# A weight conversion in two VectorE operations and a sloped ScalarE function, for three and an absolute value, in an attention and two-layer MLP kernel

## The chip, the cores and the metric

One core of a Trainium2 chip runs the whole program. The metric is the device time of one execution in microseconds (us); the median over the runs of a kernel is compared. The kernel before takes 915.51 us (three runs, 914.54 to 918.71).

## What is computed

Four batches of eight heads attend over 576 positions of width 64: the first four heads see the last 32 positions, the other four see positions that are a multiple of 32 back. The output, 2304 tokens by 512, goes through two blocks of two matrix products each (512 to 2048 to 512).

```python
attn_out = _attn_ref(q, k, v)                 # softmax over masked scores
x = attn_out as (2304, 512)
h = x @ moe_w_in
g = where(h >= 1, h, where(h <= -1, 0, (h + 1)**2 / 4))
x = g @ moe_w_out
h = x @ moe2_w_in
g = s * relu(h)**2 + b
return g @ moe2_w_out
```

The four weight matrices arrive as 64-bit floats. The core has no such type, so each weight is read as two 32-bit words and its 32-bit float is put together on chip: the high word, read as a float and multiplied by 2 to the power -112, has the right exponent bits three places too low, so that it has to be shifted left by three, and the top three bits of the low word come in below.

## The kernel before, in words

A product runs as three passes over TensorE, since each operand is a high part and a remainder (hi times hi, hi times lo, lo times hi). So each weight tile of 128 by 512 is converted to a 32-bit float (tile `wc`), then split: ScalarE copies it to the rounded type (`w_parts`, line 700, or `w_combine`, line 707, for the last matrix), and GpSimd subtracts the copy from it. There are 64 such tiles: 32 of the first block, loaded while the attention still runs, and 32 of the second, loaded late in the first block.

The conversion stands in `w_abs` (line 677) and `w_bits` (line 682). `w_abs` takes a PSUM bank `c` and lets ScalarE write |high word| times 2^-112 there. `w_bits` takes one of three buffers `wc` and issues three VectorE operations: `c` shifted left by three with the sign bit masked off, in place in PSUM; the low word shifted right by 29 and or-ed in, again in place; and the sign of the high word or-ed in, the result to `wc`. The words lie 8 bytes apart in the loaded tile `wr`.

Nothing is issued in the order of the program text. The class `Order` records every operation with a time (`nc.now`, in slots of one layer-1 or layer-2 step), and `issue` (line 267) then lays them out when the program is built: it keeps a modelled clock for each engine, and whenever an engine comes free it takes, of the operations whose inputs the model says are ready, the one with the lowest recorded time. `price` (line 228) gives the modelled duration: a VectorE operation is charged half as much per column if `fast` (line 249) holds, a scalar operation with all operands in SBUF, and `port` (line 252) says which VectorE operations the model lets wait for GpSimd's and the other way round: those that are `fast` and those with two full inputs (`whole`) in SBUF. The resulting order in each engine's queue is fixed in the program. The SyncE queue (SP), which issues nearly all DMAs, is laid out in the same way; the model lets it run at most 12 us ahead of the modelled transfers (line 354). Idle time of TensorE up to the first layer-1 step is filled, at build time, with matmuls on zeros (`idle`).

```python
        return op in ("tensor_scalar", "tensor_scalar_add", "tensor_copy") and not any(self.in_psum(x) for x in aps)
...
        return self.fast(op, aps) or len(whole) > 1
...
                free[e] = max(free[e], dma - DMA_AHEAD)
```

Around the conversions run, on VectorE, ScalarE and GpSimd: the softmax of the attention units (`s`, `mx`, `sm`, `pt`), the split of the tokens (`x_split`, line 788: `xh` by ScalarE, `xl` by VectorE or GpSimd), the activation between the layers (`activate`, line 846: `u` and `g` from the PSUM bank `h`), and the copies of a finished block of tokens (`finish`, line 957): `o` is copied from the PSUM bank `y` into one of three buffers that `u` uses as well, and SP writes it out (`x<-o`). In the second block `combine` (line 871) and `finish_fast` (line 908) do this with sums and differences of quarter blocks.

Of the kernel before, what the change touches and what calls it, by code (L numbers as in the profile page):

```python
# [12 lines left out]
F32 = mybir.dt.float32  # L13
F32R = mybir.dt.float32r
BF16 = mybir.dt.bfloat16
I32 = mybir.dt.int32
AF = mybir.ActivationFunctionType
ALU = mybir.AluOpType
# [15 lines left out]

DROP = -1.0e30

REBIAS = 2.0 ** -112

# [344 lines left out]
def attention_moe_moe(ctx, tc, q, k, v, w1_in, w1_out, w2_in, w2_out, s_in, b_in, consts, out):  # L385
    nc = Order(tc.nc)
# [268 lines left out]
    wt, wraw, wtags, reserved, used = {}, {}, {}, {}, {}  # L655

    def w_load(ph, f, x):
        w = ((w1_in, w1_out), (w2_in, w2_out))[ph][x]
        if ph == 0:
            tag = f"w{f}_{x}"  # L660
        else:
            tag = reserved[f // 2].pop(0) if x else rooms.pop(0)
        wtags[ph, f, x] = tag

        r = wraw[ph, f, x] = nc.tile(sb, [P, DM, 2], I32, tag=tag, name=f"wr{ph}_{f}_{x}")
        if x == 0:
            nc.sync.dma_start(
                out=r.rearrange("p (c m) w -> p c (m w)", m=P),
                in_=w[:, 2 * f * P:2 * (f + 1) * P].rearrange("(c p) m -> p c m", p=P),
            )  # L670
        else:
            nc.sync.dma_start(out=r.rearrange("p m w -> p (m w)"), in_=w[f * P:(f + 1) * P, :])


    wc = {}

    def w_abs(ph, f, x):
        c = nc.bank(ps, W_BANKS if now[0] < 2 * NP * NBLK - 4 else W_BANKS_FAST, f"c{ph}_{f}_{x}", "c")
        nc.scalar.activation(out=c, in_=wraw[ph, f, x][:, :, 1].bitcast(F32), func=AF.Abs, scale=REBIAS)
        wc[ph, f, x] = c  # L680

    def w_bits(ph, f, x):
        c, r = wc[ph, f, x].bitcast(I32), wraw[ph, f, x]
        o = wc[ph, f, x] = nc.tile(sb, [P, DM], I32, tag="wc", bufs=WC_BUFS, name=f"wc{ph}_{f}_{x}")
        nc.vector.tensor_scalar(
            out=c, in0=c, scalar1=3, scalar2=0x7FFFFFFF, op0=ALU.logical_shift_left, op1=ALU.bitwise_and
        )
        nc.vector.scalar_tensor_tensor(
            out=c, in0=r[:, :, 0], scalar=29, in1=c, op0=ALU.logical_shift_right, op1=ALU.bitwise_or
        )  # L690
        nc.vector.scalar_tensor_tensor(
            out=o, in0=r[:, :, 1], scalar=-0x80000000, in1=c, op0=ALU.bitwise_and, op1=ALU.bitwise_or
        )

    def w_room(tag, name, width=DM):
# [36 lines left out]
    def plan_w(f):  # L732
        for x in range(2):
            first, step, apart = W_TIMES[f // (NF // 2)]
            t = first + step * (f % (NF // 2)) + apart * x
            at(t - W_AHEAD, w_load, 0, f, x)
            at(t, w_abs, 0, f, x)
            at(t, w_bits, 0, f, x)
            at(t + 0.3, w_parts, 0, f, x)

# [6 lines left out]
    def half_split(tag):  # L747
        t = nc.tile(sb, [P, 2, 2, HM], F32R, tag=tag, name=f"halves_{tag}")
        for i in range(2):
            halves[tag, i] = t[:, i]  # L750
            half_rooms.append((tag, i))

    def pump():
        while todo and todo[0][0] <= nc.now and nc.now >= loaded[0] + W_GAP:
            ph, f, x = tile = todo[0][1]
            p = f // 2
            if x and f % 2 == 0:
                if not half_rooms and len(rooms) > 4 and p >= HP:
                    half_split(rooms.pop(0))
                if len(rooms) < 4 or not half_rooms:  # L760
                    break
                reserved[p] = [rooms.pop(0) for _ in range(4)] + [half_rooms.pop(0)]
            elif not x and not rooms:
                break
            todo.pop(0)
            loaded[0] = nc.now
            w_load(*tile)
            t = nc.now + W_AHEAD
            at(t, w_abs, *tile)
            at(t, w_bits, *tile)  # L770
            if not x:
                at(t + 0.3, w_parts, *tile)
            elif f % 2:
                at(t + 0.3, w_combine, p)
        if todo:
            at(max(nc.now + W_RETRY, todo[0][0]), pump)
# [219 lines left out]
    def at(time, fn, *args):  # L996
        heapq.heappush(events, (time, next(planned), fn, args))
# [41 lines left out]
    with tc.manual_schedule():  # L1039
# [17 lines left out]
        for f in range(NF):  # L1057
            plan_w(f)
        at(todo[0][0], pump)

        run(-1)
# [57 lines left out]
```

## Time and profile before

| | us |
|---|---|
| median of three runs (lowest, highest) | 915.51 (914.54, 918.71) |
| the profiled execution's own time | 914.73 |
| its span, first to last instruction | 913.0 |
| TensorE busy | 886.8 (97%) |
| VectorE busy | 523.3 (57%) |
| ScalarE busy | 495.9 (54%) |
| GpSimd busy | 414.1 (45%) |
| mean granted TensorE clock | 0.987 of full speed |

The busy times are sums over the span; they don't add up, since the engines run side by side. What lies outside the span (1.7 us) is start and end of the execution.

### The profile page before, as it was taken

To read this page: it belongs to the slowest core of one execution; us is meant where nothing else is said; L and a number is where in the kernel's file an instruction comes from. 1 tells how busy PE (TensorE), PEld (TensorE's weight loads), DVE (VectorE), ACT (ScalarE), POOL (GpSimd) and SP (SyncE) were. 2 spreads that over 40 slices of the span, in tenths; PEclk is the share of its full clock that TensorE was granted. 3 is DMA by queue.
4 is the path that set the end of the run, shared out by engine and by line. 5 is a ranking of instruction groups with operands and counts; after the bars stand their busy time and mean duration, and the time that the engine had idled before them with its cause. 6 is when DMAs were issued, how large, how long until landed. Compare 5 with 4: busy or idle time off the path is not lost.

```text
span 913.0 us, 22147 instructions
## 1 busy us (share of the span) xinstructions
PE 886.8 (97%) x8922; PEld 872.8 (96%) x8922; DVE 523.3 (57%) x1057; ACT 495.9 (54%) x1097; POOL 414.1 (45%) x350
## 2 busy tenths in 40 slices
PE   8987999999999999999999999999999999999996
PEld 7987999999999999999999999999999899999996
DVE  2787686443443342333696888744457965455455
ACT  2676677545444443233554687665666655555553
POOL 4174454122222112222354577987645665545544
PEclk9999799999999999999999999999999999999999
DMA  9899322422222211002635743445134332222211
GB/s 161 258 300 309 89 75 71 103 52 52 64 52 63 53 61 70 1 24 70 209 127 172 232 140 116 145 136 183 70 115 164 98 129 99 94 93 93 94 47 47
DMA packets 122966, 103.37 MB, mean 113 GB/s; under 512 B 84272, under 2 KB 100976, under 8 KB 122864
## 3 DMA queue, kind: packets, MB, share of 16 engines
q1 hardware_dynamic: 122352, 100.85, 36.7%
q0 software_dynamic: 512, 1.11, 0.6%
q8 instruction: 70, 1.15, 0.5%
q14 instruction: 32, 0.26, 0.1%
HBM read 73.63 MB, written 28.31 MB: 112 GB/s over the span
## 4 chain that ended last, share of the span: by engine, by line
PE 87%; DMA 3%; DVE 3%; ACT 2%; POOL 2%; issue 2%; SPq 0%; POOLq 0%; DVEq 0%; ACTq 0%
PE h L381 40%; PE y L381 38%; PE s L381 3%; PE o L381 2%; PE idle L381 2%; DMA wr<-in_moe_w_out_dram 1%; POOL gl L381 1%; PE t L381 1%; PE p L381 1%; DMA x<-o 1%; DMA wr<-in_moe_w_in_dram 1%; DVE o L381 1%; ACT u L381 1%; POOL w L381 1%; DMA mem<-in_q_dram 1%
## 5 line engine op out<-in xcount | busy, mean ns | idle before, releaser
L381 PE MATMUL h<-xh,w 128*128 128x256 f32 x2304 | 436.3, 281 | 5.7 <-ACT xh L381 3.0
L381 PEld LDWEIGHTS h<-xh,w 128*128 128x128 f32 x2304 | 364.0, 189 | 7.4 <-ACT xh L381 3.1
L381 PE MATMUL h<-xl,w 128*128 128x256 f32 x1152 | 323.2, 281 | 0.0
L381 PE MATMUL y<-g,w 128*128 128x256 f32 x1728 | 221.9, 283 | 5.7 <-DVE o L381 5.7
L381 PEld LDWEIGHTS h<-xl,w 128*128 128x128 f32 x1152 | 217.4, 189 | 0.3
L381 PEld LDWEIGHTS y<-g,w 128*128 128x128 f32 x1728 | 210.8, 190 | 6.6 <-DVE o L381 5.8
L381 POOL TENSOR_TENSOR g<-u,g 128x512 fp32r<-128x512 f32 x72 | 95.4, 1324 | 246.3 <-ACT g L381 148.3
L381 PE MATMUL y<-w,g 128*128 128x256 f32 x864 | 158.2, 281 | 1.0 <-ACT w L381 1.0
L381 ACT ACTIVATE u<-h 128x512 f32<-128x512 f32 x144 | 85.9, 598 | 119.0 <-DVE h L381 55.5
L381 PEld LDWEIGHTS y<-w,g 128*128 128x128 f32 x864 | 132.3, 188 | 1.3 <-ACT w L381 1.3
L381 DVE TENSOR_SCALAR u<-h 128x512 f32<-128x512 f32 x72 | 49.6, 689 | 132.1 <-PE h L381 126.7
L381 POOL TENSOR_TENSOR gl<-u,g 128x384 fp32r<-128x384 f32 x72 | 75.1, 1043 | 100.8 <-ACT g L381 95.1
L381 PE MATMUL y<-w,gl 128*128 128x256 f32 x432 | 120.7, 281 | 0.0
L381 POOL TENSOR_TENSOR gl<-s,g 128x512 fp32r<-128x512 f32 x72 | 97.8, 1358 | 33.8 <-ACT g L381 31.5
L381 ACT ACTIVATE u<-u,half 128x512 f32<-128x512 f32 x72 | 52.0, 722 | 108.2 <-DVE u L381 106.9
L381 ACT ACTIVATE g<-u 128x512 fp32r<-128x512 f32 (+1 forms) x144 | 83.2, 578 | 36.5 <-DVE u L381 30.3
L381 DVE TENSOR_SCALAR h<-h,sbt 128x512 f32<-128x512 f32 x72 | 58.6, 814 | 69.6 <-ACT h L381 69.6
L381 POOL TENSOR_TENSOR w<-wc,w 128x512 fp32r<-128x512 f32 x56 | 74.0, 1327 | 43.5 <-ACT w L381 38.8
L381 PEld LDWEIGHTS y<-w,gl 128*128 128x128 f32 x432 | 81.0, 188 | 0.1
L381 DVE TENSOR_TENSOR o<-y,o 128x256 f32<-128x256 f32 x120 | 46.4, 415 | 41.5 <-PE y L381 40.0
L381 DVE TENSOR_TENSOR u<-h,u 128x512 f32<-128x512 f32 x72 | 49.3, 685 | 23.2 <-ACT u L381 23.1
L381 ACT ACTIVATE g<-s 128x512 fp32r<-128x512 f32 x72 | 45.3, 629 | 14.8 <-DVE s L381 14.8
(91 smaller groups left out, 995.9 us busy)
## 6 DMA issues: line engine op xcount, KB each, us to landing
wr<-in_moe_w_in_dram SPq DMA_DIRECT2D x32, 512.0 KB
wr<-in_moe_w_out_dram SPq DMA_DIRECT2D x32, 512.0 KB
x<-o SPq DMA_DIRECT2D x36, 256.0 KB
scratch<-x SPq DMA_DIRECT2D x18, 512.0 KB
y<-o SPq DMA_DIRECT2D x22, 256.0 KB
scratch<-y SPq DMA_DIRECT2D x11, 512.0 KB
out_dram<-o SPq DMA_DIRECT2D x18, 256.0 KB
xhd<-xh SPq DMA_DIRECT2D x8, 512.0 KB
```

Source lines behind the costliest of these rows:

```text
L381: getattr(getattr(self.nc, engine), op)(*args, **kw)
```

## The change

ScalarE writes the high word times 2^-112 with the function Prelu, which multiplies negative values by a further factor `alpha`, here 2^32. That sets a bit of the exponent that ends up as the sign bit when the word is shifted left by three. So the sign no longer needs an operation of its own. The low word is shifted right by 29 straight into `wc`, in SBUF; and one operation shifts `c` left by three and ors the two. Nothing else is changed; `issue` lays out the whole program anew from the new operations and their modelled prices.

```diff
-REBIAS = 2.0 ** -112
+REBIAS, SIGN = 2.0 ** -112, 2.0 ** 32
...
-    def w_abs(ph, f, x):
+    def w_high(ph, f, x):
         c = nc.bank(ps, W_BANKS if now[0] < 2 * NP * NBLK - 4 else W_BANKS_FAST, f"c{ph}_{f}_{x}", "c")
-        nc.scalar.activation(out=c, in_=wraw[ph, f, x][:, :, 1].bitcast(F32), func=AF.Abs, scale=REBIAS)
+        nc.scalar.activation(out=c, in_=wraw[ph, f, x][:, :, 1].bitcast(F32), func=AF.Prelu, scale=REBIAS, alpha=SIGN)
         wc[ph, f, x] = c
 
     def w_bits(ph, f, x):
-        c, r = wc[ph, f, x].bitcast(I32), wraw[ph, f, x]
+        c = wc[ph, f, x].bitcast(I32)
         o = wc[ph, f, x] = nc.tile(sb, [P, DM], I32, tag="wc", bufs=WC_BUFS, name=f"wc{ph}_{f}_{x}")
-        nc.vector.tensor_scalar(
-            out=c, in0=c, scalar1=3, scalar2=0x7FFFFFFF, op0=ALU.logical_shift_left, op1=ALU.bitwise_and
-        )
+        nc.vector.tensor_scalar(out=o, in0=wraw[ph, f, x][:, :, 0], scalar1=29, scalar2=None, op0=ALU.logical_shift_right)
         nc.vector.scalar_tensor_tensor(
-            out=c, in0=r[:, :, 0], scalar=29, in1=c, op0=ALU.logical_shift_right, op1=ALU.bitwise_or
-        )
-        nc.vector.scalar_tensor_tensor(
-            out=o, in0=r[:, :, 1], scalar=-0x80000000, in1=c, op0=ALU.bitwise_and, op1=ALU.bitwise_or
+            out=o, in0=c, scalar=3, in1=o, op0=ALU.logical_shift_left, op1=ALU.bitwise_or
         )
...
-            at(t, w_abs, 0, f, x)
+            at(t, w_high, 0, f, x)
...
-            at(t, w_abs, *tile)
+            at(t, w_high, *tile)
```

## Rows read from the trace of the kernel before

**Rows 1.** The page's busy times of each engine: us, share of the span, instructions.

```profile
PE 886.8 (97%) x8922; PEld 872.8 (96%) x8922; DVE 523.3 (57%) x1057; ACT 495.9 (54%) x1097; POOL 414.1 (45%) x350
```

**Rows 2.** Busy time by stretch: stretch, its length, busy of each engine, clock, DMA.

```profile
40.00:50.00 10.00, 6.31 (x119) 5.33 (x118) 7.63 (x13) 7.55 (x18) 5.44 (x5) 1.00 1.10 346
50.00:60.00 10.00, 9.89 (x71) 9.58 (x69) 9.98 (x17) 7.68 (x14) 7.50 (x6) 0.83 1.12 312
...
80.00:90.00 10.00, 6.14 (x50) 5.43 (x48) 7.09 (x13) 5.08 (x10) 4.20 (x5) 0.87 0.99 258
90.00:100.00 10.00, 7.16 (x92) 6.87 (x93) 6.60 (x12) 4.45 (x9) 3.74 (x3) 0.50 0.31 110
...
100.00:700.00 600.00, 598.72 (x6076) 590.88 (x6075) 335.19 (x636) 321.84 (x760) 256.08 (x211) 1.00 0.34 101
700.00:750.00 50.00, 46.49 (x386) 45.41 (x385) 41.99 (x93) 30.39 (x57) 32.31 (x26) 1.00 0.28 95
```

**Rows 3.** Waits, TensorE's and one of ScalarE's: total us, times, longest.

```profile
PE y L381 <- DVE o L381: 6.1, 2, 5.7
PE h L381 <- ACT xh L381: 3.0, 1, 3.0
ACT c L381 <- DMA wr<-in_moe_w_out_dram: 8.3, 3, 5.8
```

**Rows 4.** Groups of instructions, the conversion of one weight tile: count | busy us, mean ns.

```profile
L381 DVE SCALAR_TENSOR_TENSOR c<-wr,c 128x512 int32<-128x512 int32 x64 | 43.4, 687 | 0.3
L381 DVE TENSOR_SCALAR c<-c 128x512 int32<-128x512 int32 x64 | 43.3, 691 | 15.0 <-ACT c L381 15.0
L381 DVE SCALAR_TENSOR_TENSOR wc<-wr,c 128x512 int32<-128x512 int32 x64 | 42.9, 677 | 1.6 <-POOL w L381 1.2
L381 ACT ACTIVATE c<-wr 128x512 f32<-128x512 f32 x64 | 39.7, 632 | 14.2 <-DMA wr<-in_moe_w_out_dram 8.3 <-DMA wr<-in_moe_w_in_dram 5.8
```

**Rows 5.** Groups of instructions: operations of other kinds that bound the new ones.

```profile
L381 DVE CAST narrow<-wide 128x310 bf16<-128x310 f32 x1 | 0.3, 325 | 2.6 <-DMA wide<-in_const_dram 2.6
L381 DVE TENSOR_TENSOR xl<-scratch,xh 128x512 fp32r<-128x512 f32 x9 | 12.4, 1382 | 0.6 <-ACT xh L381 0.6
L381 DVE TENSOR_TENSOR xl<-xr,xh 128x512 fp32r<-128x512 f32 x10 | 7.2, 736 | 1.2 <-ACT xh L381 1.2
L381 POOL TENSOR_TENSOR w<-wc,w 128x512 fp32r<-128x512 f32 x56 | 74.0, 1327 | 43.5 <-ACT w L381 38.8 <-DMA wr<-in_moe_w_in_dram 3.3 <-DMA wr<-in_moe_w_out_dram 1.3
L381 ACT ACT_TABLE_LOAD x1 | 1.3, 1283 | 0.7 <-PEq L1102 0.7
```

**Rows 6.** The chain that ended last, 36 to 92 us: start, us, what.

```profile
36.01 5.50 PE idle L381 x46
...
42.30 0.67 DVE wc L381
42.97 0.68 DVE c L381 x2
...
44.09 0.69 DVE c L381
...
83.71 8.36 DMA x<-o
```

**Rows 7.** Instructions in order of time, SP's queue and VectorE's, 71 to 92 us.

```profile
71.27 0.68 DVE L381 COPY o<-y 128x512 f32<-128x512 f32 x1
...
81.04 1.06 SPq L381 DMA_DIRECT2D wr<-in_moe_w_out_dram  x1
...
83.71 9.96 SPq L381 DMA_DIRECT2D x<-o  x4
...
92.09 0.69 DVE L381 COPY o<-y 128x512 f32<-128x512 f32 x1 [4.74 <-DMA x<-o]
```

**Rows 8.** Instructions in order of time, VectorE and TensorE, 716 to 718 us.

```profile
716.79 0.68 DVE L381 SCALAR_TENSOR_TENSOR wc<-wr,c 128x512 int32<-128x512 int32 x1
...
717.82 0.36 PE L381 MATMUL h<-xh,w 128*128 128x256 f32 x1 [1.70 <-DVE s L381]
```

## The prediction

> **What bounds the kernel now.** I read the page's busy times first, then busy time by stretch, TensorE's waits, and the chain that ended last where those pointed. TensorE is busy 886.8 of 913.0 us [rows 1], so there are 26.2 us of idle time to win, and VectorE, at 523.3 us, bounds nothing over the whole. The reader is to look for the stretches in which TensorE stands still while weights are being converted. There are three: 40 to 50 us, with 10.00 - 6.31 = 3.69 us; 80 to 100 us, with 20.00 - 6.14 - 7.16 = 6.70 us; and 700 to 750 us, with 50.00 - 46.49 = 3.51 us [rows 2]. From 100 to 700 us, where most weights are converted, it is 600.00 - 598.72 = 1.28 us [rows 2]; the other 11 us lie in the first 20 and the last 15, where none is.
>
> The waits name the causes [rows 3]. In the first stretch TensorE waits 3.0 us for a split token block (`xh`, ScalarE). In the second it waits 5.7 us for VectorE's copy `o`. In the third the longest wait is for VectorE's `s`, 1.70 us at 717.82 [rows 8]. TensorE's clock belongs to the price: 0.83 in 50 to 60 us and 0.50 in 90 to 100 us, each after an idle stretch [rows 2]; 0.50 is the lower of its two levels, 1.2 GHz.
>
> What ends these waits matters more. The chain goes through fillers (5.50 us) until the first layer-1 step and then through four conversion pieces, 0.67 + 0.68 + 0.69 = 2.04 us [rows 6]; here VectorE is in the way. The wait of the second stretch is not VectorE's: the copy at 92.09 us itself waited 4.74 us for a DMA that frees its buffer, `x<-o`, which stood in SP's queue behind weight loads and was issued at 83.71, though its data were copied at 71.27 [rows 7]; the transfer then took 8.36 us [rows 6]. At 717 us a conversion of 0.68 us stands in VectorE's queue just ahead of the `s` that TensorE waits for [rows 8].
>
> **The change part by part.** *ScalarE.* One operation on the same 512 columns stays one, from the loaded words to PSUM. Abs takes 632 ns [rows 4]; no row shows the sloped function. The nearest is Abs, and I take the same, change 0. Were it a tenth slower, 64 x 0.06 = 4 us would be spread over an engine at 54%; a gain of as much is the other end.
>
> *VectorE, removed.* Per tile 691 + 687 + 677 = 2055 ns [rows 4], 64 times 131.5 us.
>
> *VectorE, added.* The or of two words reads one operand in PSUM and one in SBUF, as the two removed ones did: 0.68 us. The shift from SBUF to SBUF has no row. The lower bound is the CAST between SBUF tiles, 325 ns for 310 columns [rows 5]; stretched in proportion to 512 it is 0.54. The upper one is the removed operation's 0.69 plus what an operation loses that meets GpSimd: the same subtraction with both inputs in SBUF takes 736 ns from `xr`, and 1382 ns from `scratch`, when GpSimd works beside it [rows 5]; the difference is 0.65, so 1.34. GpSimd is busy 5.44 and 7.50 of 10 us in the first stretches [rows 2], with subtractions of 1327 ns that belong to this very conversion [rows 5]. I take 0.45 for the shift, between 0.33 and 0.54, and half a meeting, 0.33: 0.78. A tile then costs 0.78 + 0.68 = 1.46 for 2.06 us, a gain of 0.60, or 38 us of 523 over 64 tiles. The ends: 0.33 + 0.68 gives 67 us, 1.34 + 0.69 gives 2 us.
>
> The Trainium skill (SBUF — State Buffer, "SBUF: two separate sides") has a rule against this change: a VectorE operation that uses both port pairs and a GpSimd operation lock each other out for a whole instruction, where the removed operations, with one operand in PSUM, need no lock. The pair 736 and 1382 agrees for operations with two inputs; for a shift with one input no row shows it. By that rule the 2 us end is the nearer one in busy stretches; without it the gain would be about 131.5 - 64 x 1.13 = 59 us.
>
> *The order in time.* The shift no longer waits for ScalarE, only for the load and for a `wc` buffer, and may run beside ScalarE. Behind the load there stand 0.63 + 0.68 us on the path, for 0.63 + 2.06. The PSUM bank is held for two VectorE operations fewer. In exchange `wc` is held longer, and VectorE takes over the wait on the load, with all that is queued behind it.
>
> *What of this reaches the end.* Most of the 38 us is covered by TensorE itself, which stands still for only 1.28 us in the 600 us that hold most conversions [rows 2]; without that cover they would count in full. Three places remain.
> - First layer-1 step, 36 to 49 us. The first weight comes earlier by up to 2.06 - 0.68 = 1.4 us; the four pieces on the chain shrink by a third, 0.7 us, and the wait of 3.0 us is the cap on what else can go. Bounds 0 and 1.4 + 3.0 = 4.4; I take 2, the two small pieces. Late next are the attention's own copies.
> - 87 to 92 us. If SP's order stays, the 2 us are lost here, since `x<-o` lands at 92.07 whatever VectorE does. The order is computed anew, though, and data that are ready earlier move the write ahead of a load or two (each issue takes about 1 us of SP, such as 1.06 [rows 7]). I count half: 1 us kept. Bounds: 0, and 2 plus all of the stall.
> - 700 to 750 us. 3.51 us of idle time [rows 2], 1.70 of it behind a queue that loses 0.60 per tile [rows 8]. I take 1.5, bounds 0 and 3.5.
>
> Sum: 1 + 1.5 = 2.5 us off the profiled execution's own 914.73, or 912.2. This lies 0.8 under the median of the runs shown; for a median I take 912.5.
>
> **The rivals.** *The stall at 87 us goes, by half or more.* The write is laid out ahead of the loads and TensorE doesn't stop. For it: the data are ready 12 us before the issue, and the model's VectorE gets faster, which pulls the write forward. Against it: all loads of the first block have earlier chances, and nothing in the change touches SP. It gives 6.7 us of idle time, and of the cold 90 to 100 us half of 7.16, 3.6: 912.5 - 10.3 = 902 if all of it goes, 907 if half.
>
> *VectorE inherits the load's wait.* Today ScalarE waits for loads, in one case 5.8 us [rows 3]. The shift comes first in the new order; laid out by modelled landing times, and a load landing late, it stops VectorE, with the activation of the running block queued behind it (`u`, then `g`, for which TensorE waits). For it: loads do land late, three times for 8.3 us, and GpSimd may hold the shift as well. Against it: the removed first operation was just as stuck behind ScalarE's, 0.63 us later, and TensorE did not stop then. It decides where the load is late by more than the layer step that TensorE has in hand, 24 matmuls, an estimated 24 x 46.49 / 386 = 2.9 us [rows 2]. Price: that wait uncovered, nothing gained: 915.5 + 5.8 = 921.
>
> *Nothing shows.* The DMA landing absorbs the start and other VectorE work the late stretch: 915.
>
> *The sloped function is in another table.* The page shows one ACT_TABLE_LOAD of 1283 ns for the whole program [rows 5], so Abs, Exp, Copy, Square and Relu share a set. If Prelu were outside, up to 64 x 2 loads, 164 us, would fall on ScalarE; even a quarter uncovered gives 955. The Trainium skill (ScalarE: Activation LUTs, "Table sets: the hidden batching unit") says that cheap functions are in every set; it doesn't list this one.
>
> **How the numbers follow.** Chances: forecast 0.39 (its own range 909 to 914.5), nothing shows 0.19, the stall goes 0.20, the inherited wait 0.18, the table 0.04. A measurement of this kernel can tell about 0.5%, 4.6 us, from no change. Faster by more is the stall's 0.20 and the better part of the forecast, bounds of the start kept whole (4.4 + 3.5 = 7.9 at most), 0.14: 0.34. Slower is the table and most of the inherited wait, 0.16: 0.20. The rest, 0.46, is within. Both larger rivals are needed for 8 in 10: the range is 902 to 920, which leaves out the table, a stall that takes more with it, and the worst of the wait, about 0.15.
>
> **What would show it.** Right: VectorE's busy time falls to about 485 us, the conversion groups are two with 0.68 and some 0.8 us, `c` on ScalarE stays at 632 ns, one table load; the first layer-1 step comes before 41 us, and TensorE's idle time in 40 to 50 and 700 to 750 us falls. Wrong: `x<-o` issued well before 83 us, with no stall near 87; or TensorE waiting for VectorE's `u` or `wc` where it didn't; or a shift of 1.3 us, with which VectorE is no lighter.

## The result and the profile after

The changed kernel takes **904.57 us** (median of four runs, 900.9 to 906.37) against 915.02 us for the kernel before in the same comparison (four runs, 911.76 to 918.71): a ratio of 0.9882, 95% interval 0.9856 to 0.9908, or 10.4 us faster. The forecast was 912.5, with 902 to 920 as its range. The profiled execution is the quickest of the four, 900.9 us with a span of 899.1; so the two profiled executions lie 13.8 us apart (914.73 and 900.9) where the medians lie 10.4 apart. What is read from one trace each may be some 3 us too favourable to the change.

The page's busy times, to be held against [rows 1]:

```profile
PE 878.1 (98%) x8904; PEld 865.6 (96%) x8904; DVE 488.2 (54%) x993; ACT 496.1 (55%) x1097; POOL 418.0 (46%) x350
```

VectorE lost 64 operations and 35.1 us. TensorE, with the same matmuls of the program to do and 18 fillers fewer, lost 8.7 us of busy time, and its idle time went from 26.2 to 899.1 - 878.1 = 21.0 us. The busy time by stretch [rows 2] says where (stretch, its length, busy us of PE, PEld, DVE, ACT, POOL, TensorE's granted clock, DMA):

```profile
40.00:50.00 10.00, 7.14 (x109) 6.28 (x109) 5.90 (x7) 9.28 (x20) 6.46 (x5) 0.69 1.13 314
50.00:60.00 10.00, 8.58 (x70) 8.24 (x69) 8.50 (x15) 8.00 (x15) 7.11 (x6) 0.97 1.01 279
...
80.00:90.00 10.00, 7.52 (x126) 6.97 (x124) 5.57 (x12) 7.61 (x16) 6.77 (x5) 1.00 1.02 313
90.00:100.00 10.00, 10.00 (x117) 9.74 (x118) 6.57 (x13) 6.70 (x18) 5.11 (x4) 1.00 0.52 130
100.00:700.00 600.00, 597.84 (x6053) 591.01 (x6052) 315.81 (x610) 322.38 (x755) 257.74 (x212) 1.00 0.34 101
700.00:750.00 50.00, 49.09 (x413) 48.66 (x413) 33.03 (x77) 29.36 (x55) 32.02 (x26) 1.00 0.31 107
```

The reader is to look at 80 to 100 us. Idle time there was 3.86 + 2.84 = 6.70 us, and it is now 2.48; and the clock in 90 to 100 us, 0.50 before, is 1.00. Before, TensorE was busy for 7.16 us of that slice at half clock [rows 2], so 3.58 us more were lost; the lower clock of 80 to 90 us (0.87 over the slice) fell into time in which it stood still and cost nothing more. The whole loss of the two slices was 6.70 + 3.58 = 10.3 us and is now 2.5. The matmul that ended the stall, before and after, in order of time (start, us, engine, out<-in, and in brackets the idle time before and who ended it):

```profile
92.84 2.29 PE L381 MATMUL y<-g,w 128*128 128x256 f32 x9 [5.73 <-DVE o L381]
```

```profile
89.99 0.85 PE L381 MATMUL y<-g,w 128*128 128x256 f32 x5 [2.38 <-DVE o L381]
```

TensorE's waits after the change show the same place [rows 3]:

```profile
PE h L381 <- ACT xh L381: 2.8, 1, 2.8
PE y L381 <- DVE o L381: 2.4, 1, 2.4
PE p L381 <- DVE s L381: 1.7, 1, 1.7
...
PE h L381 <- DVE s L381: 0.5, 1, 0.5
```

The wait for the copy `o` fell from 5.7 to 2.4 us, the two waits of `h` for `s`, one of them the 1.70 at 717.82 [rows 8], shrank to one of 0.5, and the wait for `xh` in the first stretch is nearly what it was (2.8 for 3.0). The groups of the conversion [rows 4, 5] (count | busy us, mean ns | idle time before them):

```profile
L381 POOL TENSOR_TENSOR w<-wc,w 128x512 fp32r<-128x512 f32 x56 | 77.0, 1383 | 41.4 <-ACT w L381 39.3 <-PE y L381 1.4 <-PE h L381 0.3
...
L381 DVE TENSOR_SCALAR wc<-wr 128x512 int32<-128x512 int32 x64 | 52.6, 839 | 10.6 <-DMA wr<-in_moe_w_out_dram 4.0 <-POOL w L381 3.4 <-DMA wr<-in_moe_w_in_dram 3.2
...
L381 DVE SCALAR_TENSOR_TENSOR wc<-c,wc 128x512 int32<-128x512 int32 x64 | 43.1, 680 | 2.1 <-ACT c L381 1.6
...
L381 ACT ACTIVATE c<-wr 128x512 f32<-128x512 f32 x64 | 40.1, 635 | 15.8 <-DMA wr<-in_moe_w_out_dram 8.2 <-DMA wr<-in_moe_w_in_dram 7.4
...
L381 ACT ACT_TABLE_LOAD x1 | 1.3, 1283 | 0.7 <-PEq L1097 0.7
```

Three operations with 2055 ns became two with 839 + 680 = 1519. Prelu takes 635 ns, as Abs did, and there is one table load. VectorE now does wait for loads, 4.0 + 3.2 us over the run. The chain that ended last, with the start of layer 1 [rows 6] (start, us, what):

```profile
35.70 2.98 PE idle L381 x25
38.69 0.24 PE h L381 x2
```

The first layer-1 matmul starts at 38.69; in the kernel before, the fillers ahead of it ended at 36.01 + 5.50 = 41.51 [rows 6]. Last, the instructions in order of time around the copy of the first finished tokens [rows 7]:

```profile
66.93 0.68 DVE L381 COPY o<-y 128x512 f32<-128x512 f32 x1
...
74.63 2.55 POOL L381 TENSOR_TENSOR w<-wc,w 128x512 fp32r<-128x512 f32 x2 [2.12 <-ACT w L381]
75.96 2.96 DVE L381 TENSOR_SCALAR wc<-wr 128x512 int32<-128x512 int32 x2 [0.52 <-POOL w L381]
77.14 1.51 POOL L381 TENSOR_TENSOR g<-u,g 128x512 fp32r<-128x512 f32 x1
...
78.92 0.79 SPq L381 DMA_DIRECT2D x<-o  x1
79.75 0.43 SPq L381 DMA_DIRECT2D wr<-in_moe_w_out_dram  x1
...
80.78 1.51 SPq L381 DMA_DIRECT2D x<-o  x1
82.34 0.96 SPq L381 DMA_DIRECT2D wr<-in_moe_w_out_dram  x2
...
89.24 0.69 DVE L381 COPY o<-y 128x512 f32<-128x512 f32 x1 [2.80 <-POOL g L381]
```

The first copy comes 4.3 us earlier (66.93 for 71.27). Its two writes `x<-o` now stand among the last weight loads, at 78.92 and 80.78, instead of behind them at 83.71; and the next copy, at 89.24, waits for GpSimd's `g` and no longer for the DMA that frees its buffer.

### The profile page after: what moved, and what is told of

The parts are those of the page before. It is cut to its first block, busy times and chain, and to the rows that moved or that the text cites. A ratio compares the mean times of both kernels' runs of the same rounds, so it can differ in the third digit from the quotient of the medians.

```text
span 899.1 us, 22027 instructions
## 1 busy us (share of the span) xinstructions
PE 878.1 (98%) x8904; PEld 865.6 (96%) x8904; DVE 488.2 (54%) x993; ACT 496.1 (55%) x1097; POOL 418.0 (46%) x350
## 4 chain that ended last, share of the span: by engine, by line
PE 91%; DMA 2%; DVE 2%; SPq 2%; ACT 1%; issue 1%; POOL 0%; DVEq 0%; POOLq 0%; ACTq 0%
PE h L381 44%; PE y L381 41%; PE s L381 2%; PE o L381 2%; SPq L381 2%; DMA wr<-in_moe_w_out_dram 1%; PE p L381 1%; DMA raw<-in_k_dram 1%; DVE o L381 1%; PE idle L381 1%; DVE wc L381 1%; PE t L381 0%; DMA mem<-in_q_dram 0%; ACT u L381 0%; DVE xl L381 0%
## 5 line engine op out<-in xcount | busy, mean ns | idle before, releaser
L381 POOL TENSOR_TENSOR w<-wc,w 128x512 fp32r<-128x512 f32 x56 | 77.0, 1383 | 41.4 <-ACT w L381 39.3
L381 DVE TENSOR_SCALAR wc<-wr 128x512 int32<-128x512 int32 x64 | 52.6, 839 | 10.6 <-DMA wr<-in_moe_w_out_dram 4.0
```

The lines of the kernel that those rows point to most:

```text
L381: getattr(getattr(self.nc, engine), op)(*args, **kw)
```

## The experiments

The question was which of three things gained the 10 us: the shorter conversion where it stands, the order of the program (which is laid out anew for the new operations), or only the place of those two writes in SP's queue. Of each edit the lines that matter are shown; `...` marks a cut. "The planner" is the part of the program that lays out the order when it is built (`issue`, with the durations of `price`). Ratios are against runs of the kernel before on the same chip, whose medians were 914.5, 914.74 and 914.59 us.

**1. Operations and order apart.** First the new operations in the old order: the planner still sees the old ones, so that every instruction keeps its place, and both new ones are put where the third stood.

```diff
...
+                if "emit" in kw:
+                    for o, k in kw["emit"]:
+                        getattr(getattr(self.nc, engine), o)(**{x: self.real(y) for x, y in k.items()})
+                    continue
...
-            out=o, in0=r[:, :, 1], scalar=-0x80000000, in1=c, op0=ALU.bitwise_and, op1=ALU.bitwise_or
+            out=o, in0=r[:, :, 1], scalar=-0x80000000, in1=c, op0=ALU.bitwise_and, op1=ALU.bitwise_or, emit=[
+                ("tensor_scalar", dict(out=o, in0=r[:, :, 0], scalar1=29, scalar2=None, op0=ALU.logical_shift_right)),
+                ("scalar_tensor_tensor", dict(
+                    out=o, in0=c, scalar=3, in1=o, op0=ALU.logical_shift_left, op1=ALU.bitwise_or)),
+            ],
...
```

> The order of the kernel before, as it was laid out for three operations, but with the changed operations put in: Prelu for Abs, and shift and or, together, where the third operation stood. Theory 1 (the gain comes from the new order, above all from where the write x<-o stands in SP's queue): x<-o is still issued at about 83 us behind four loads, the wait of some 6 us near 87 us stays, and the time is 912 to 916 us. Theory 2 (the gain is VectorE's shorter work itself): most of the gain is there, 904 to 908 us. Either way VectorE's busy time falls by 30 to 40 us against the kernel before.

Measured: 921.72 us, ratio 1.0068 (1.0045 to 1.0091). It is slower, which neither theory had said; and VectorE's busy time fell by 26 us, to 497.1, not by the 30 to 40 that both had.

Then the reverse, the old three operations in the new order, all three where the new kernel has its or (the same hook, with the lists exchanged).

> The order of the changed kernel, as it was laid out for two operations, but with the three operations of before (and Abs), all three where the or stood. Theory 1 (order): near the changed kernel, 904 to 909 us, though VectorE is busy 523 us again. Theory 2 (VectorE's work): the gain is gone, 913 to 918 us.

Measured: 927.5 us, ratio 1.0141 (1.0107 to 1.0175). With operations that take longer than it was laid out for, and with all three at one place, the new order is the slowest kernel of all. So the order by itself brings no gain to the old operations; what it would be worth without those two burdens, this run can't tell.

The first of the two had a flaw: `wc` is complete later when both operations come third. So the shift was put where the second operation stood, wherever the earlier reader of its buffer has been issued by then.

```diff
+                if "early" in kw and early(i):
+                    kw["emit"] = [kw["early"]]
+                if "late" in kw:
+                    kw["emit"] = kw["late"][early(i - 1):]
...
```

> The changed operations (Prelu, shift, one shift-and-or) in the layout of the kernel before, as in the run with both new operations at the third operation's place, but the shift now stands at the second operation's place wherever the wc buffer's earlier reader has been issued by then, so that wc is ready no later than before. Theory 1 (a lighter VectorE is worth little by itself; the gain is that the whole order is laid out anew for it): 911 to 916, VectorE's conversion near 97 us, the first-pass writes still issued near 84 us, the wait PE y<-DVE o still 4 us or more. Theory 2 (the lighter VectorE gives the gain wherever its work stands): 903 to 908 and that wait under 2.5. If it stays at 920, the late wc of the first run was not what made it slow; the longer shift beside GpSimd would be next.

Measured: 918.34 us, ratio 1.0033 (1.0019 to 1.0048): 2 us above the range of the first theory, and far from the second; TensorE's wait for the copy `o` is still there, 5.9 us, as the first theory said. VectorE is as light here as in the changed kernel (busy 488.0 us, of which the conversion takes 44.4 + 43.7 = 88.1). Why the kernel is slower than before, and not level with it, stays open. Busy time by stretch, and VectorE's copy in order of time:

```profile
80.00:90.00 10.00, 6.00 (x52) 5.62 (x50) 4.39 (x8) 5.30 (x10) 4.71 (x5) 0.92 1.01 281
90.00:100.00 10.00, 7.52 (x94) 7.23 (x94) 5.48 (x12) 4.77 (x9) 3.94 (x3) 0.50 0.27 91
700.00:750.00 50.00, 46.31 (x362) 45.56 (x361) 38.83 (x85) 29.47 (x55) 30.95 (x26) 0.93 0.22 79
```

```profile
83.12 10.19 SPq L394 DMA_DIRECT2D x<-o  x4
...
91.74 0.69 DVE L394 COPY o<-y 128x512 f32<-128x512 f32 x1 [6.26 <-DMA x<-o]
```

This copy is the plainest reading of the study. In the kernel before it waited 4.74 us for the DMA and began at 92.09 [rows 7]; with a lighter VectorE it waits 6.26 and begins at 91.74. What VectorE saves ahead of a copy that hangs on a transfer turns into waiting. 90 to 100 us is at clock 0.50 as before, and 700 to 750 us has gained nothing either: 3.69 us of idle time for 3.51, and a clock of 0.93 for 1.00.

**2. The place of the writes alone.** In the kernel before, only the two first writes were moved ahead, one before four and one before two of the last loads; in the changed kernel, the reverse, both behind all four.

```diff
...
+        for x, loads in zip(at_name["x2_0_0"], (("wr0_13_1", "wr0_15_0"), ("wr0_14_1", "wr0_15_1"))):
+            for k, name in enumerate(loads, 1):
+                start[at_name[name][0]] = start[x] + 1e-4 * k
...
```

> The kernel before with one thing moved: the two writes x<-o of the first pass stand ahead of two and four of the last four weight loads in SP's queue, as they do in the changed kernel, in place of behind all four. Nothing else differs. Theory 1 in its narrow form (these two writes): they land some 5 us earlier, the wait near 87 us shrinks from 5.7 to 2 us or less, the clock stays up, and the time falls by 4 to 9 us, to 906 to 911. If it is VectorE's work, or the order of everything else: 913 to 916.

Measured: 908.34 us, ratio 0.9929 (0.9908 to 0.995). Moving two loads behind each of two writes, with the old operations, gains 6.2 us, as the narrow form of the first theory had it. SP's queue, VectorE's copy, and the stretches:

```profile
80.99 1.07 SPq L392 DMA_DIRECT2D x<-o  x1
...
83.19 0.45 SPq L392 DMA_DIRECT2D x<-o  x1
...
87.04 0.68 DVE L392 COPY o<-y 128x512 f32<-128x512 f32 x1
```

```profile
80.00:90.00 10.00, 8.15 (x59) 7.22 (x57) 9.76 (x18) 5.68 (x12) 3.99 (x4) 0.89 1.08 275
90.00:100.00 10.00, 10.00 (x174) 9.70 (x174) 6.21 (x13) 8.10 (x20) 6.33 (x5) 0.94 0.64 169
700.00:750.00 50.00, 46.49 (x385) 45.40 (x384) 38.57 (x87) 30.15 (x56) 32.58 (x27) 1.00 0.31 107
```

The copy no longer waits, it begins 5 us earlier, and the clock of 90 to 100 us is 0.94. The last stretch is as before, 46.49: that part of the gain does not come with the writes.

Now the changed kernel with both writes last:

```diff
...
+        moved = at_name["x2_0_0"]
+        for k, x in enumerate(moved, 1):
+            start[x] = start[at_name["wr0_15_1"][0]] + 1e-4 * k
...
```

> The changed kernel with the two writes x<-o of the first pass moved behind the last four weight loads, where they stood before. Theory 1 in its narrow form: the wait near 87 us comes back, and the time rises by 4 to 9 us, to 909 to 914. If it is VectorE's work, or the order of everything else: 903 to 907, no change.

Measured: 904.67 us, ratio 0.9886 (0.9863 to 0.9908), the same as the changed kernel to 0.1 us. Here the copy waits for something else first (VectorE's, then ScalarE's):

```profile
90.86 0.69 DVE L390 COPY o<-y 128x512 f32<-128x512 f32 x1 [2.77 <-POOL g L390]
92.23 0.60 ACT L390 ACTIVATE o<-y 128x512 f32<-128x512 f32 x1 [3.47 <-DMA x<-o]
```

So the late writes cost 6 us in the old layout and, in the median, nothing in the new one. In the profile they do cost something where they stand: 80 to 100 us loses 4.8 us for 2.5, and the clock of 90 to 100 us is 0.83; the profiled executions are the quickest of each kernel, 903.25 and 900.9. The place of the writes is one way to lose the time, not the cause of the whole gain.

**3. Another layout for the same operations.** The planner's prices were changed by hundredths of a us, which rearranges the whole program and leaves every operation as it is. Over 63 such sets of prices (VectorE's, ScalarE's and GpSimd's fixed parts) the planner's own end lies between 869.0 and 882.4 for the old operations and between 860.1 and 875.6 for the new; with the prices as they stand it is 875.7, the median of its 63, for the kernel before, and 863.0, one of the shortest, for the changed one. These are a plan's numbers, not times; five layouts were run.

```diff
-            return 0.15 + (0.00052 if self.fast(op, aps) else 0.00104) * n
+            return 0.13 + (0.00052 if self.fast(op, aps) else 0.00104) * n
```

> The kernel before with its own three operations; only the planner's price of a VectorE operation is lowered from 0.15 to 0.13 us of fixed part, so that the whole order is laid out anew. In this layout the first-pass writes come ahead of the last weight loads, and the planner's own end falls by 6 us (875.7 to 869.5). Theory 1 (much of the gain is where this one layout happened to fall, and any layout with the writes early has it): 906 to 910, wait PE y<-DVE o under 2.5. Theory 2 (the gain needs the shorter conversion): 913 to 917.

Measured: 909.01 us, ratio 0.9931 (0.9907 to 0.9955): 5.7 us gained with the old operations, the time of the first theory. Its mechanism is not there, though: the writes, issued at 82.79, have just one load behind them, not several as the expectation has it, and TensorE still waits 3.6 us for a copy `o` (ScalarE's), not under 2.5. The loss between 80 and 100 us still falls from 10.3 to 6.3 us, in the account below.

With 0.14 instead:

> The kernel before with its own three operations, laid out anew with the planner's fixed VectorE price at 0.14 us for 0.15: planner's end 873.2 against 875.7, first-pass writes behind all four last weight loads as before. Theory 1 (a layout is worth some us either way whatever the operations, and the shorter conversion some us on top): 910 to 914, with a stall near 85 to 90 us still in the waits. Theory 2 (the changed operations alone make the gain and the relaid kernel with 909 was the exception): 914 to 917.

Measured: 913.76 us, ratio 0.9987 (0.9971 to 1.0004), no difference from the kernel before that could be told. The value lies in the range of the first theory, and TensorE's wait for the copy is there, 4.3 us.

The longest plan (VectorE 0.17, ScalarE 0.16, GpSimd 0.26):

> The kernel before with its own three operations, laid out anew with fixed prices that give the longest of 63 planned ends with these operations, 882.4 against 875.7 (VectorE 0.17 for 0.15, ScalarE from PSUM 0.16 for 0.17, GpSimd 0.26 for 0.25). Theory 1 (the layout moves the time, and the planner's end says in which direction): 917 to 922. Theory 2 (the time follows the operations, not the layout): 913 to 916, whatever the planner says.

Measured: 916.13 us, ratio 1.001 (0.9996 to 1.0025), between the ranges of the two theories and no difference that could be told; the plan's 6.7 us more became 1.5 on the chip.

The changed kernel with 0.155:

> The changed kernel with its own operations; only the planner's fixed price of a VectorE operation is raised from 0.15 to 0.155 us, so that the order is laid out anew. In this layout the first-pass writes stand behind the last weight loads, as before, and the planner's own end is 875.6, 12.6 above that of the changed kernel and level with the kernel before. Theory 1 (much of the gain is where this one layout happened to fall): 911 to 917, with the wait PE y<-DVE o or its like back at 3 us or more. Theory 2 (the gain belongs to the shorter conversion, whatever the layout): 903 to 908.

Measured: 907.9 us, ratio 0.9916 (0.9899 to 0.9933). This is the time of the second theory: a plan no better than that of the kernel before, and still 6.8 us under it. The wait that the first theory named is back all the same, 3.3 us for ScalarE's copy `o`. The changed kernel with its shortest plan (0.13, 0.18, 0.24):

> The changed kernel with its own operations, laid out anew with fixed prices that give the shortest of 63 planned ends with these operations, 860.1 against 863.0 (VectorE 0.13 for 0.15, ScalarE from PSUM 0.18 for 0.17, GpSimd 0.24 for 0.25); first-pass writes among the last weight loads. Theory 1 (the planner's end says the direction): 899 to 903, below the changed kernel. Theory 2 (the planner's end and the chip do not go together at this size, as in the relaid changed kernel with 907.9 at a planned 875.6): 904 to 909.

Measured: 903.48 us, ratio 0.9872 (0.9847 to 0.9897), between the two ranges, and 1.1 us under the changed kernel where the plan says 2.9; within what can be told apart, no difference.

**4. Two operations without the form from SBUF to SBUF.** Both read `c` in PSUM: one shifts it in place, one shifts the low word and ors.

```diff
...
-        nc.vector.tensor_scalar(out=o, in0=wraw[ph, f, x][:, :, 0], scalar1=29, scalar2=None, op0=ALU.logical_shift_right)
+        nc.vector.tensor_scalar(out=c, in0=c, scalar1=3, scalar2=None, op0=ALU.logical_shift_left)
         nc.vector.scalar_tensor_tensor(
-            out=o, in0=c, scalar=3, in1=o, op0=ALU.logical_shift_left, op1=ALU.bitwise_or
+            out=o, in0=r[:, :, 0], scalar=29, in1=c, op0=ALU.logical_shift_right, op1=ALU.bitwise_or
         )
```

> Two operations and Prelu as in the changed kernel, but neither is the SBUF-to-SBUF form: the first shifts c left by 3 in PSUM, the second shifts the low word right by 29 and ors c into it, writing wc. Laid out anew by the planner; its first-pass writes come among the last weight loads as in the changed kernel. VectorE's conversion 64 x (0.69 + 0.68) = about 88 us against 95.7. Theory 1 (two operations for three is the gain, the form of the shift is not): 903 to 907, no VectorE group of the conversion above 0.72 us mean. Theory 2 (the short SBUF form, which can start before ScalarE has written c, is what the order needs): 909 to 915, with more idle time of GpSimd or PE behind VectorE's wc.

Measured: 905.12 us, ratio 0.989 (0.987 to 0.991), as fast as the changed kernel. Its groups, and VectorE's copy in order of time:

```profile
L381 DVE SCALAR_TENSOR_TENSOR wc<-wr,c 128x512 int32<-128x512 int32 x64 | 43.0, 676 | 2.5 <-POOL w L381 1.5
L381 DVE TENSOR_SCALAR c<-c 128x512 int32<-128x512 int32 x64 | 43.0, 689 | 14.1 <-ACT c L381 14.1
```

```profile
89.11 0.69 DVE L381 COPY o<-y 128x512 f32<-128x512 f32 x1 [5.21 <-DMA x<-o]
```

The shift that waits for ScalarE's `c` and takes 689 ns does as well as the one that needn't wait and takes 839. This kernel has most of the loss of 80 to 100 us left, 8.1 of 10.3 us in the account below: its copy waits 5.21 us for the transfer although the writes are issued at 80.20, and it gains its time elsewhere. And with its shortest plan (VectorE 0.155, ScalarE 0.18, GpSimd 0.26):

> The form with both operations from PSUM, laid out anew with fixed prices that give the shortest of 63 planned ends with that form, 862.1 against 866.7 (VectorE 0.155 for 0.15, ScalarE from PSUM 0.18 for 0.17, GpSimd 0.26 for 0.25); first-pass writes among the last weight loads. Theory 1 (the planner's end says the direction): 899 to 903, below both the changed kernel and the first run of this form. Theory 2 (they do not go together at this size): 904 to 908.

Measured: **901.07 us**, ratio 0.9853 (0.9822 to 0.9884), the lowest median of the study and within the range of the first theory; its interval overlaps that of the changed kernel. Its copy and its stretches:

```profile
77.47 0.93 SPq L381 DMA_DIRECT2D x<-o  x2
...
86.80 0.69 DVE L381 COPY o<-y 128x512 f32<-128x512 f32 x1 [1.37 <-DMA x<-o]
```

```profile
80.00:90.00 10.00, 8.78 (x134) 8.08 (x133) 7.53 (x14) 6.92 (x15) 5.32 (x4) 1.00 1.06 389
90.00:100.00 10.00, 10.00 (x120) 9.78 (x119) 6.40 (x11) 7.95 (x26) 5.14 (x4) 1.00 0.65 166
700.00:750.00 50.00, 48.52 (x411) 48.14 (x410) 32.16 (x80) 29.99 (x57) 31.46 (x27) 1.00 0.30 106
```

**All profiles in one account.** For every kernel, the time in which TensorE ran no matmul of the program was added up (it stood idle, or ran nothing but fillers; there are 24.3 us of these before and 21.4 after, all in the first 60 us), and half of the time in which it ran one at the lower clock. The lower clock counts only while TensorE is busy: idle time is lost once, whatever the clock. What is left of the span is the program's matmuls at full clock. It is 857 to 861 us in all fourteen profiles, so these losses are what differs between them, to within 4 us.

| us lost in | 0 to 60 | 60 to 80 | 80 to 100 | 100 to 700 | 700 to 750 | 750 to end | span | left |
|---|---|---|---|---|---|---|---|---|
| before | 30.7 | 0.0 | 10.3 | 1.8 | 3.5 | 7.1 | 913.0 | 859.5 |
| before, 0.14 | 33.1 | 0.0 | 7.7 | 1.1 | 2.5 | 7.1 | 910.4 | 858.9 |
| before, longest plan | 30.2 | 0.0 | 6.0 | 5.6 | 4.0 | 7.1 | 912.9 | 860.0 |
| before, 0.13 | 31.5 | 0.0 | 6.3 | 1.2 | 3.9 | 7.1 | 908.2 | 858.2 |
| before, writes ahead | 30.3 | 0.0 | 3.6 | 1.5 | 3.5 | 7.1 | 906.1 | 860.1 |
| new operations, old order, both third | 32.8 | 0.0 | 8.9 | 3.8 | 9.7 | 7.1 | 920.8 | 858.5 |
| the same, shift early | 31.1 | 0.0 | 10.2 | 3.0 | 7.1 | 7.1 | 916.7 | 858.2 |
| old operations, new order | 32.7 | 3.7 | 5.6 | 14.2 | 2.5 | 9.4 | 928.8 | 860.8 |
| after | 29.1 | 0.0 | 2.5 | 2.2 | 0.9 | 7.1 | 899.1 | 857.4 |
| after, writes behind | 30.7 | 0.0 | 4.8 | 0.5 | 0.9 | 7.2 | 901.4 | 857.3 |
| after, 0.155 | 33.6 | 1.3 | 6.1 | 0.0 | 0.9 | 7.2 | 906.0 | 856.8 |
| after, shortest plan | 30.1 | 0.0 | 4.9 | 1.1 | 0.4 | 7.1 | 901.7 | 858.1 |
| both from PSUM | 28.1 | 0.0 | 8.1 | 0.0 | 1.5 | 7.1 | 902.7 | 857.9 |
| the same, shortest plan | 29.2 | 0.0 | 1.2 | 0.6 | 1.5 | 7.4 | 897.8 | 858.0 |

Two things can be read from it. From 700 to 750 us every layout of its own with two operations loses 0.4 to 1.5 us, and every layout with three 2.5 to 4.0 (one profile each): about 2.5 us belong to the conversion, in whichever of these layouts. From 80 to 100 us the values are 6.0 to 10.3 with three operations laid out by the planner and 1.2 to 8.1 with two: the means are 7.6 (four layouts) and 4.6 (five), but the two ranges overlap: each single value depends on where a layout happens to put things.

## Why the prediction was right and wrong

*The number.* The main forecast, 912.5 with its own range of 909 to 914.5, was missed: the kernel gained 10.4 us, not 2.5 to 3. The time lies within 902 to 920 because the first rival was counted into that range. The profiled executions differ by 13.9 us of span; in the account 1.6 of it fall to the first 60 us, 7.8 to 80 to 100 us and 2.6 to 700 to 750 us, 0.4 go the other way from 100 to 700 us, and 2.1 lie in what is left, with no place.

*What was costed rightly.* The shift was put at 0.78 us and measures 0.839, the or at 0.68 and measures 0.680; VectorE's 485 us are 488.2. Prelu costs what Abs did (635 against 632 ns), with one table load, so the rival of the other table is out.

*GpSimd and the shift.* In order of time above, two shifts at 75.96 take 2.96 us together while GpSimd works from 74.63 to 74.63 + 2.55 and from 77.14 to 77.14 + 1.51. The view of the tile `wc` gives min, median and max in ns and the first and the last start, here and in the run with the old order and the early shift:

```profile
L381 DVE TENSOR_SCALAR wc<-wr x64: 408/692/1541, 33.0 to 713.4; 128x512 int32<-128x512 int32 x64
```

```profile
L390 DVE TENSOR_SCALAR wc<-wr x64: 364/424/1529, 35.4 to 730.8; 128x512 int32<-128x512 int32 x64
```

The times of single instructions in the trace of the changed kernel settle it: 22 of the 64 shifts overlap no GpSimd instruction and take 419 ns on average (408 to 428); the other 42 take 1058 on average, up to 1541. A meeting costs 0.64 us, where the prediction had 0.65, a free shift 0.42 for its 0.45, and two shifts in three meet GpSimd, where it had one in two. The Trainium skill (SBUF — State Buffer, "SBUF: two separate sides") has the rule that GpSimd and a VectorE operation that uses both port pairs shut each other out for a whole instruction. These times agree with it for a shift with one input. The meetings cost the mean shift its whole advantage over the 0.689 us from PSUM, and GpSimd's subtraction takes 1383 ns for 1327.

*The start.* The term was 2 us. Layer 1 starts 2.8 us earlier, and the loss of the first 60 us fell from 30.7 to 29.1, by 1.6. Right in size; the fillers fell by 2.9 us (24.3 to 21.4), while idle time in these 60 us rose from 7.5 to 8.3. The wait for `xh` (2.8) stayed, as the term assumed.

*700 to 750 us.* The term was 1.5, with 3.5 as its bound; it measures 2.6. The waits for `s`, 2.2 us of this stretch, are gone from it. But it isn't the shorter queue ahead of one `s`, as the term had it: with the shorter operations in the old order (the early shift) the waits for `s` there are 2.4 us, and the stretch lost 7.1, not 3.5. The gain comes with an order in which the last operation of the last conversion starts at 714.2 us, where before it started at 729.2.

*87 to 92 us: the step that failed.* The prediction kept 1 us of the start past the stall and gave the stall itself nothing. It measures 10.3 - 2.5 = 7.8 us between the two traces. The case was there as the first rival, "the stall at 87 us goes, by half or more"; its price for all of it, 6.7 + 3.6 = 10.3 us, is what the stretch lost, and three quarters of that went. Its chance, 0.20, was too small, and the time came out at 904.57, between its 902 and 907. The argument against it, that "nothing in the change touches SP", was wrong: in this program the order of all queues comes out of one plan, and the data of the first write, ready some 5 us earlier in it (4.3 on the chip, 66.93 for 71.27), let the first write be laid out ahead of four loads and the second ahead of two. What stood right in the sentence before ("data that are ready earlier move the write ahead of a load or two") should have had the weight. What the rival had too simply is that the writes' place decides: behind all loads the changed kernel takes the same time (904.67), and the form from PSUM is as fast with the writes early and most of the loss left.

*The inherited wait.* VectorE does wait for loads now (4.0 + 3.2 us), and TensorE waits 1.4 us for `u`, where it had waited 0.4; it was not the bound. *Nothing shows* is excluded by the interval, which ends at 0.9908.

*What is shown, and what is not.* Shown: the new operations in the old order gain nothing (1.0033 and 1.0068); the new order with the old operations bunched at one place loses (1.0141); an order of their own lets the old operations have from -0.7% to +0.1% and the new ones from -0.8% to -1.3%. The means are (914.6 + 913.8 + 916.1 + 909.0) / 4 = 913.4 and (904.6 + 907.9 + 903.5) / 3 = 905.3: some 8 us for the conversion, give or take 3 to 4 us for where a layout falls. With four and three layouts, picked by hand (the longest plan of the old operations, the longest and the shortest of the new) and not drawn, that split is an estimate. Which of the many shifted instructions makes one layout better than another between 80 and 100 us was settled for one pair only, the writes of the kernel before.

## What to carry to other kernels

In a program whose order is planned from modelled durations, a shorter operation is worth what a new plan makes of it: cost the plan's own moves, in every queue, and try two or three neighbouring plans of both kernels before a few us are put down to the operation. Where TensorE is 97% busy, count its idle time, half of its busy time at the lower clock, and its fillers, slice by slice, with no moment counted twice: here the three together held the differences between fourteen spans to within 4 us, and 6.7 us of idle time cost 10.3. Taking work from an engine that then waits for a transfer gains nothing at that place: look at the bracket behind the copy, not at the engine's busy share.

## What the hardware showed that was not expected

The VectorE shift from SBUF to SBUF takes 364 to 408 ns at its quickest for 512 32-bit words that lie 8 bytes apart, against 689 for the shift in PSUM; beside GpSimd up to 1541. On average it was the slower of the two (839), and the kernel with the PSUM form has GpSimd's subtractions at 1322 ns where the changed kernel has them at 1383.
